# VectorE's order at the start of a fused attention and feed-forward block: tile 1's scaled x and tile 6's statistics change places

## The chip, the cores and the metric

The kernel runs on one core of a Trainium2 chip. The metric is the device time of one execution in microseconds (us), as the median of several timed runs. One more execution is recorded by the hardware profiler; its rows are the source of every other time below. The engines are called as the profile calls them: PE (TensorE, matrix products), DVE (VectorE), ACT (ScalarE), POOL (GpSimd) and SP (SyncE, which here only issues DMAs). PEld is the loading of weights into PE. Every engine works through its own list of instructions in order, and waits where an operand of another engine or of a DMA has not been signalled yet.

## The reference: what is computed

The input x has 2048 rows (tokens) of 512 values, in bfloat16. It is normalised over each row, and two branches of the normalised rows are added to x:

```python
xn = (x - mean(x)) / sqrt(var(x) + 1e-5)
# A: linear attention, 32 heads of 16
q, k, v = split(xn @ wqkv)                     # wqkv 512 x 1536
phi = lambda t: where(t > 0, t + 1, exp(t)) + 1e-6
kv  = sum over tokens of phi(k)^T v            # per head, 16 x 16
z   = sum over tokens of phi(k)
o   = phi(q) kv / (phi(q) . z + 1e-6)
A   = o @ wo                                   # wo 512 x 512
# B: gated feed-forward
B   = (silu(xn @ w_gate) * (xn @ w_up)) @ w_down   # inner width 1792
out = x + A + B
```

## The kernel before, in words

The 2048 rows are 16 tiles of 128 rows (`t` = 0 to 15). There are three stages. In the first, the head and a loop over tiles, every tile gets its statistics (mean and variance), its normalised rows, its k and q products, and the feature phi(k), called `pk`; a running product of xn and `pk` over all tiles is kept in four banks of the PE's accumulator memory (`gtacc`, L624). In the second, those sums are turned into the matrices that attention needs. In the third, the feed-forward products and the output tiles are worked through, in four chunks of 512 rows. The change touches the head alone, which ends near 17 us of 209.6; the loop over tiles from 5 on follows it.

Nothing plans the order. A small class, `_Prog`, keeps one list per engine: each call of a helper appends instructions to the list of its engine, in the order in which the calls stand in the source, and works out from the names read and written which semaphores must be waited for. So the order of calls in the source, written out by hand, is the order in which each engine works.

The helpers that matter here, by engine:

- DVE: `bns(t)` (L299) takes a tile's statistics and `agg(t)` (L302) makes mean and variance of them (`mv`). `xc_full(t)` (L426) subtracts the mean from x. `xn_dve(t)` (L316) makes the scaled x, that is (x - mean) * rstd, for tile t (`xn_sb`); `xn(t)` is the same followed, for t of 3 and more, by a DMA transpose of it on SP's queue (L463), which gives `xnT`. `clip_k(t)` (L539) clips the exponential of k. `first_feat(t)` (L588) adds it to the positive part `kpos` and writes the feature `pk`; for tiles from 4 on `maxadd_k(t)` (L548) does this from the accumulator bank.
- POOL: `eps(t)` and `rstd_of(t)` (L327, L336) add the epsilon to the variance and raise it to the power of -1/2; `eps_two(t)` and `rstd_two(t)` (L344, L353) do so for tiles t and t+1 in one instruction each. `feat_pool(0)` (L581) writes tile 0's feature, and `zsum(t)` (L612 for tile 0, L616 for the others) adds up the features over tiles, in float32.
- ACT: `first_ek`, `first_pk` and `first_pq` (L556, L562, L574) read the products of the first four tiles from the banks, scaled by `rstd`, as exponential of k, positive part of k (`kpos`) and q; `exp_k` (L520) is the exponential from tile 4 on.
- PE: `proj_part` and `proj_first` (L499, L486) form the products of the first four tiles, whose x is only centred and not scaled; `kproj` and `qproj` (L472) those of tiles 4 to 15, from `xnT`; `gtacc(t)` (L624) needs tile t's scaled x as weights and its feature as the other operand.

x arrives in single tiles up to tile 5, and in pairs from tile 6 on (6 and 7 together, then 8 and 9, and so on). Two waits are put into POOL's list on purpose: `zsum(0, [("xn", 3)])` starts only after tile 3's scaled x, and `zsum(1, [("xn", 7)])` only after tile 7's.

Of the kernel before, what the change touches and what calls it, by code (L numbers as in the profile page):

```python
# [109 lines left out]
def bass_parallel_sum__linear_attn_block__swiglu_ffn__prompt_kernel(  # L110
# [13 lines left out]
    pe, act, dve, pool, sp = nc.tensor, nc.scalar, nc.vector, nc.gpsimd, nc.sync  # L124
    bf, f32 = dt.bfloat16, dt.float32

    with contextlib.ExitStack() as es:
# [76 lines left out]
        def xload(eng, h, t0, n, after=()):  # L204
            K.dma(
                eng, lambda: h.dma_start(x_sb[:, t0:t0 + n, :], rows(xin, t0, n)),
                r=list(after), w=[("x", t0 + i) for i in range(n)],
            )
# [89 lines left out]
        def bns(t):  # L298
            K.op("dve", lambda: dve.bn_stats(stats[:, t, :], x_sb[:, t, :]), r=[("x", t)], w=[("st", t)])  # L299

        def agg(t):
            K.op("dve", lambda: dve.bn_aggr(mv[:, t, :], stats[:, t, :]), r=[("st", t)], w=[("mv", t)])  # L302
# [10 lines left out]
        def xn_dve(t):  # L313
            K.op(
                "dve",
                lambda: dve.tensor_scalar(  # L316
                    out=xn_sb[:, t, :], in0=x_sb[:, t, :], scalar1=mv[:, t, 0:1], scalar2=rstd[:, t:t + 1],
                    op0=ALU.subtract, op1=ALU.mult,
                ),
                r=[("x", t), ("mv", t), ("rstd", t)], w=[("xn", t)],  # L320
            )

        def eps(t, eng):
            h = dve if eng == "dve" else pool
            K.op(
                eng,
                lambda: h.tensor_scalar(  # L327
                    out=vpe[:, t:t + 1], in0=mv[:, t, 1:2], scalar1=1e-5, scalar2=None, op0=ALU.add,
                ),
                r=[("mv", t)], w=[("vpe", t)],  # L330
            )

        def rstd_of(t):
            K.op(
                "pool",
                lambda: pool.tensor_tensor(out=rstd[:, t:t + 1], in0=vpe[:, t:t + 1], in1=nhalf[:, 0:1], op=ALU.pow),  # L336
                r=[("vpe", t), ("nhalf",)], w=[("rstd", t)],
            )

        def eps_two(t, eng):  # L340
            h = dve if eng == "dve" else pool
            K.op(
                eng,
                lambda: h.tensor_scalar(  # L344
                    out=vpe[:, t:t + 2], in0=mv[:, t:t + 2, 1], scalar1=1e-5, scalar2=None, op0=ALU.add,
                ),
                r=[("mv", t), ("mv", t + 1)], w=[("vpe", t), ("vpe", t + 1)],
            )

        def rstd_two(t):  # L350
            K.op(
                "pool",
                lambda: pool.tensor_tensor(  # L353
                    out=rstd[:, t:t + 2], in0=vpe[:, t:t + 2], in1=nhalf[:, :], op=ALU.pow,
                ),
                r=[("vpe", t), ("vpe", t + 1), ("nhalf",)], w=[("rstd", t), ("rstd", t + 1)],
            )
# [65 lines left out]
        def xc_full(t):  # L423
            K.op(
                "dve",
                lambda: dve.tensor_scalar(  # L426
                    out=xc_sb[:, t, :], in0=x_sb[:, t, :], scalar1=mv[:, t, 0:1], scalar2=None, op0=ALU.subtract,
                ),
                r=[("x", t), ("mv", t)], w=[("xc", t, 0), ("xc", t, 1)],
            )  # L430
# [29 lines left out]
        def transpose_dma(t):  # L460
            K.dma(
                "sp",
                lambda: sp.dma_start_transpose(out=xnT[:, :, t * P:(t + 1) * P], in_=xn_sb[:, t, :]),  # L463
                r=[("xn", t)], w=[("xnT", t)],
            )
# [15 lines left out]
        def proj_first(t, wname, h):  # L481
            lo, b = (D, kb(t)) if wname == "wk" else (0, qb(t))
            K.op(
                "pe",
                [
                    (lambda c=c: pe.matmul(  # L486
                        banks[b], xcT[:, NDC * t + c, :], wqkv_sb[:, c, lo:lo + D],
                        start=(c == 0), stop=(c == NDC - 1),
                    ))
                    for c in (2 * h, 2 * h + 1)  # L490
                ],
                r=[("xcT", t, i) for i in (2 * h, 2 * h + 1)] + [(wname, i) for i in (2 * h, 2 * h + 1)], w=[bk(b)],
            )

        def proj_part(t, wname, c, pos):
            lo, b = (D, kb(t)) if wname == "wk" else (0, qb(t))
            K.op(
                "pe",
                lambda: pe.matmul(  # L499
                    banks[b], xcT[:, NDC * t + c, :], wqkv_sb[:, c, lo:lo + D],  # L500
                    start=(pos == 0), stop=(pos == NDC - 1),
                ),
                r=[("xcT", t, c), (wname, c)], w=[bk(b)],
            )
# [49 lines left out]
        def first_ek(t):  # L554
            K.op(
                "act", lambda: act.activation(ek[:, t % NE, :], banks[kb(t)], ACT.Exp, scale=rstd[:, t:t + 1]),  # L556
                r=[bk(kb(t)), ("rstd", t)], w=[("ek", t % NE)],
            )

        def first_pk(t):  # L560
            K.op(
                "act", lambda: act.activation(kpos[:, t % NE, :], banks[kb(t)], ACT.Relu, scale=rstd[:, t:t + 1]),  # L562
                r=[bk(kb(t)), ("rstd", t)], w=[("kpos", t % NE)],
            )
# [7 lines left out]
        def first_pq(t):  # L572
            K.op(
                "act", lambda: act.activation(pkq[:, t, 1, :], banks[qb(t)], ACT.Identity, scale=rstd[:, t:t + 1]),  # L574
                r=[bk(qb(t)), ("rstd", t)], w=[("pq", t)],
            )
# [15 lines left out]
        def clip_k(t):  # L592
            clip(ek[:, t % NE, :], ("ek", t % NE))
# [14 lines left out]
        def zsum(t, after=()):  # L608
            pk = pkq[:, t, 0, :]
            after = list(after)  # L610
            if t == 0:
                K.op("pool", lambda: pool.tensor_copy(zacc[:, :], pk), r=[("pk", t)] + after, w=[("zacc",)])  # L612
            else:
                K.op(
                    "pool",
                    lambda: pool.tensor_tensor(out=zacc[:, :], in0=zacc[:, :], in1=pk, op=ALU.add),  # L616
                    r=[("pk", t), ("zacc",)] + after, w=[("zacc",)],
                )

        def gtacc(t):  # L620
            K.op(
                "pe",
                [
                    (lambda c=c: pe.matmul(  # L624
                        banks[4 + c], xn_sb[:, t, c * P:(c + 1) * P], pkq[:, t, 0, :],
                        start=(t == 0), stop=(t == NT - 1),
                    ))
                    for c in range(NDC)
                ],
                r=[("xn", t), ("pk", t)], w=[bk(4 + c) for c in range(NDC)],  # L630
            )
# [7 lines left out]
        def xn(t):  # L639
            xn_dve(t)  # L640
            if t >= 3:
                transpose_dma(t)
# [35 lines left out]
        first_ek(0)  # L678
        clip_k(0)
        xc_full(3)  # L680
        bns(4)
        proj_part(1, "wk", 0, 0)
        proj_part(1, "wk", 1, 1)
# [14 lines left out]
        agg(4)  # L698
        bns(5)
        agg(5)  # L700
        bns(6)
        agg(6)
        proj_part(0, "wq", 2, 2)
        proj_part(1, "wq", 2, 2)
        proj_part(0, "wq", 3, 3)
# [1 line left out]
        proj_part(1, "wq", 3, 3)  # L707
        proj_first(2, "wk", 0)
        proj_first(2, "wk", 1)
        eps_two(1, "pool")  # L710
        rstd_two(1)
        first_ek(1)
        clip_k(1)
        first_pq(1)
# [3 lines left out]
        gtacc(0)  # L718
        eps_two(3, "pool")
        rstd_two(3)  # L720
        eps_two(5, "pool")
        rstd_two(5)
        xn(4)
        xload("sp", sp, 12, 2)
        xn_dve(1)
        first_pk(1)
        first_feat(1)
        proj_first(3, "wk", 0)
# [5 lines left out]
        first_pk(2)  # L734
        first_feat(2)
        xn(5)
        xn(6)
        first_pq(2)
        proj_first(3, "wk", 1)
        first_ek(3)  # L740
# [3 lines left out]
        gtacc(1)  # L744
        gtacc(2)
        xn_dve(3)
        zsum(0, [("xn", 3)])
        bns(7)
        kproj(4)
# [374 lines left out]
```

## Time and profile before

| | |
|---|---|
| median of 3 timed runs | 210.42 us (210.40 to 210.62) |
| profiled execution, whole time | 210.88 us |
| its span, first to last instruction | 209.6 us |
| busy share of the span: PE, DVE, ACT, POOL | 99%, 57%, 34%, 34% |
| granted PE clock | 1.00 |

The profile's span begins with the first instruction; all positions are us from there. The whole time of the profiled execution has 1.28 us around the span. A row of the timeline gives the start, the length, the engine, the line of the kernel, the operation, the tile written and the tiles read, the shapes, and the count of instructions in the row; one row can hold several instructions of one kind that follow each other. A bracket at its end tells how long the engine had been idle before and what ended that. Instructions of DVE and ACT overlap a little: the next one starts some 0.08 us before the one ahead has been written out, so that the distance between two starts is shorter than the length. A PE row's end is modelled, and the distance of starts is the better measure there too.

### The profile page before, as it was taken

Reading aid. Unit: us, or ns where it says so; the run is one execution under the profiler, and the core shown is the slowest. Engines: PE = TensorE matmul, PEld = TensorE weight load, DVE = VectorE, ACT = ScalarE, POOL = GpSimd, SP = SyncE. Lnnn points to the kernel's source line nnn. Section 1 sums busy time; section 2 is a strip of 40 time slices with the busy share of each in tenths; the row PEclk is TensorE's granted clock in tenths of the full one; section 3 lists DMA queues with packets and bytes.
Section 4 is the critical chain, followed back from the end, with each engine's and each line's share of the span. In section 5 each row is a group of like instructions: output and inputs, shape, how many; then the busy total and the mean of one; then the engine's idle time right before and its main releaser. Section 6 shows DMA issues by size and latency. Waiting matters only on the chain.

```text
span 209.6 us, 2822 instructions
## 1 busy us (share of the span) xinstructions
PE 206.9 (99%) x1014; PEld 94.5 (45%) x1014; DVE 120.3 (57%) x246; ACT 71.3 (34%) x126; POOL 72.0 (34%) x90
## 2 busy tenths in 40 slices
PE   8999999999999999999999999999999999999996
PEld 3444444444444444444444444444444444444444
DVE  4989989335465874637355746365556535374122
ACT  6686666976543331302122312213031213121000
POOL 3526977658032443223141422240424132221200
DMA  6763644697797021010101110102011010110101
GB/s 201 225 179 71 127 78 100 175 377 240 192 359 68 2 46 26 29 25 25 50 2 50 28 25 25 50 0 53 2 48 25 27 28 25 46 32 25 50 28 50
DMA packets 30287, 16.84 MB, mean 80 GB/s; under 512 B 20928, under 2 KB 29632, under 8 KB 30272
## 3 DMA queue, kind: packets, MB, share of 16 engines
q1 hardware_dynamic: 29984, 16.39, 29.9%
q10 hardware_dynamic: 288, 0.26, 0.4%
q8 instruction: 8, 0.13, 0.3%
q14 instruction: 7, 0.06, 0.1%
HBM read 9.70 MB, written 2.10 MB: 56 GB/s over the span
## 4 chain that ended last, share of the span: by engine, by line
PE 97%; DMA 1%; DVE 1%; issue 0%
PE psum L821 46%; PE psum L1026 23%; PE psum L472 10%; PE psum L1015 7%; PE psum L624 7%; PE psum L499 2%; PE psum L486 2%; DMA x_sb<-in_A_x_dram 1%; PE psum L444 0%; DVE stats L299 0%; PE psum L928 0%; PE psum L410 0%; PE psum L951 0%; DVE xc_sb L380 0%; DVE out_sb L1039 0%
## 5 line engine op out<-in xcount | busy, mean ns | idle before, releaser
L836 ACT ACTIVATE sg<-psum 128x512 bf16<-128x512 f32 x56 | 33.4, 598 | 106.0 <-PE psum L821 103.6
L821 PE MATMUL psum<-xnT,wg_sb 128*128 128x512 bf16 x224 | 57.5, 379 | 0.0
L821 PE MATMUL psum<-xnT,wu_sb 128*128 128x512 bf16 x224 | 57.5, 379 | 0.0
L970 POOL TENSOR_TENSOR prod<-pkq,zb 128x512 f32<-128x512 bf16 x16 | 18.6, 1161 | 55.9 <-DVE pkq L548 55.9
L821 PEld LDWEIGHTS psum<-xnT,wu_sb 128*128 128x128 bf16 x224 | 21.9, 98 | 26.4
L821 PEld LDWEIGHTS psum<-xnT,wg_sb 128*128 128x128 bf16 x224 | 21.7, 98 | 26.2 <-issue 0.2
L1039 DVE TENSOR_TENSOR out_sb<-psum,x_sb 128x512 bf16<-128x512 f32 (+2 forms) x17 | 11.2, 660 | 35.9 <-PE psum L1026 35.9
L994 POOL TENSOR_TENSOR pqn<-pkq,rden 128x512 bf16<-128x512 bf16 x16 | 16.9, 1055 | 36.6 <-DVE rden L988 36.6
L842 DVE TENSOR_TENSOR pkq<-psum,sg 128x512 bf16<-128x512 f32 x28 | 19.2, 686 | 17.1 <-PE psum L821 14.7
L842 DVE TENSOR_TENSOR xn_sb<-psum,sg 128x512 bf16<-128x512 f32 x28 | 18.8, 671 | 14.2 <-PE psum L821 13.6
L1026 PE MATMUL psum<-wd_sb,xn_sb 128*128 128x512 bf16 (+2 forms) x126 | 25.7, 355 | 0.0
L1026 PE MATMUL psum<-wd_sb,pkq 128*128 128x512 bf16 x112 | 25.5, 379 | 0.0
L472 PE MATMUL psum<-wqkv_sb,xnT 128*128 128x512 bf16 x96 | 22.5, 379 | 0.0
L616 POOL TENSOR_TENSOR zacc<-zacc,pkq 128x512 f32<-128x512 f32 x15 | 17.3, 1155 | 5.0 <-DVE ek L539 4.6
L1026 PEld LDWEIGHTS psum<-wd_sb,xn_sb 128*128 128x128 bf16 x126 | 11.8, 98 | 12.5
L1026 PEld LDWEIGHTS psum<-wd_sb,pkq 128*128 128x128 bf16 x112 | 11.0, 98 | 13.2
L1015 PE MATMUL psum<-m_sb,eq 128*128 128x512 bf16 (+2 forms) x68 | 16.6, 366 | 0.0
L624 PE MATMUL psum<-pkq,xn_sb 128*128 128x512 bf16 x64 | 15.9, 379 | 0.0
L472 PEld LDWEIGHTS psum<-wqkv_sb,xnT 128*128 128x128 bf16 x96 | 9.4, 98 | 11.3
L978 DVE TENSOR_REDUCE den<-prod 128x32 f32<-128x512 f32 x16 | 10.9, 683 | 5.9 <-POOL prod L970 5.9
L299 DVE BATCH_NORM_STATS2 stats<-x_sb 128x6 f32<-128x512 bf16 x16 | 10.9, 679 | 3.3 <-DMA x_sb<-in_A_x_dram 3.3
L548 DVE SCALAR_TENSOR_TENSOR pkq<-pkq,eq 128x512 bf16<-128x512 bf16 x16 | 11.1, 693 | 0.6
(73 smaller groups left out, 139.3 us busy)
## 6 DMA issues: line engine op xcount, KB each, us to landing
out_dram<-out_sb SPq DMA_DIRECT2D x15, 128.0 KB, 1.7
wg_sb<-in_B_w_gate_dram SPq DMA_DIRECT2D x2, 896.0 KB, 8.2
wu_sb<-in_B_w_up_dram SPq DMA_DIRECT2D x2, 896.0 KB, 6.4
wd_sb<-in_B_w_down_dram SPq DMA_DIRECT2D x1, 1792.0 KB, 11.1
x_sb<-in_A_x_dram SPq DMA_DIRECT2D x5, 256.0 KB, 3.0
x_sb<-in_A_x_dram SPq DMA_DIRECT2D x5, 128.0 KB, 3.2
wqkv_sb<-in_A_wqkv_dram SPq DMA_DIRECT2D x5, 128.0 KB, 3.4
wqkv_sb<-in_A_wqkv_dram SPq DMA_DIRECT2D x1, 512.0 KB, 8.4
```

What stands on the lines that cost most here:

```text
L472: (lambda c=c: pe.matmul(banks[b], xnT[:, c, t * P:(t + 1) * P], wqkv_sb[:, c, lo:lo + D], start=(c == 0), stop=(c == NDC - 1),))
L548: lambda: dve.scalar_tensor_tensor(out=dst, in0=src, scalar=0.0, in1=e, op0=ALU.max, op1=ALU.add,),
L616: lambda: pool.tensor_tensor(out=zacc[:, :], in0=zacc[:, :], in1=pk, op=ALU.add),
L624: (lambda c=c: pe.matmul(banks[4 + c], xn_sb[:, t, c * P:(c + 1) * P], pkq[:, t, 0, :], start=(t == 0), stop=(t == NT - 1),))
L821: (lambda c=c: pe.matmul(banks[b], w_sb[:, c, fc * P:(fc + 1) * P], xnT[:, c, C * 512:(C + 1) * 512], start=(c == 0), stop=(c == NDC - 1),))
L836: lambda: act.activation(sg[:, j % NSG, :], banks[gb], ACT.Silu),
L842: lambda: dve.tensor_tensor(out=hT(C, fc), in0=banks[ub], in1=sg[:, j % NSG, :], op=ALU.mult,),
L970: lambda: pool.tensor_tensor(out=p, in0=pkq[:, t, 1, :], in1=zb[:, :], op=ALU.mult),
L994: lambda: pool.tensor_tensor(out=pqn[:, t % NPN, :].rearrange("p (i g h e) -> p g i h e", i=NB, g=NG, e=DH), in0=pkq[:, t, 1, :].rearrange ...
L1015: (lambda g=g: pe.matmul(dst, pqnT(t)[:, g, :], m_sb[:, g, lo:hi], start=(g == 0), stop=False,))
L1026: (lambda fc=fc: pe.matmul(dst, hT(C, fc)[:, jj * P:(jj + 1) * P], wd_sb[:, fc, lo:hi], start=False, stop=(fc == NFC - 1),))
L1039: lambda: dve.tensor_tensor(out=o, in0=src, in1=x_sb[:, t, lo:hi], op=ALU.add),
```

## The change

Four calls or groups of calls in the head move; no instruction's shape changes except that the factors of tiles 5 and 6, formed by one pair of POOL instructions on two tiles, become two pairs on one tile each.

- Tile 1's scaled x, `xn_dve(1)`, stood behind tile 4's scaled x. It now stands behind `xc_full(3)`. The factors that it needs, `eps_two(1)` and `rstd_two(1)`, are called just ahead of it; POOL's own order is not changed by that, since no other POOL call stands between the two places.
- Tile 6's statistics, `bns(6)` and `agg(6)`, stood behind those of tile 5. They now stand behind the features of tiles 1 and 2 and tile 5's scaled x, ahead of `clip_k(3)`.
- Tile 6's factor is formed there as well, by `eps(6)` and `rstd_of(6)`, and tile 5's by `eps(5)` and `rstd_of(5)` at the place where both were formed together.
- Tile 6's scaled x and its transpose, `xn(6)`, stood behind `xn(5)`. They now stand behind tile 3's scaled x, ahead of the statistics of tile 7.

DVE's list in that part, by tile (s statistics and aggregate, c centred x, x scaled x, k clip, f feature):

```
before: c3 s4 s5 s6 k1 x4 x1 f1 k2 x2 f2 x5 x6 k3 f3 x3 s7
after:  c3 x1 s4 s5 k1 x4 f1 k2 x2 f2 x5 s6 k3 f3 x3 x6 s7
```

```diff
--- before.py
+++ after.py
@@ -678,6 +678,9 @@
         first_ek(0)
         clip_k(0)
         xc_full(3)
+        eps_two(1, "pool")
+        rstd_two(1)
+        xn_dve(1)
         bns(4)
         proj_part(1, "wk", 0, 0)
         proj_part(1, "wk", 1, 1)
@@ -698,8 +701,6 @@
         agg(4)
         bns(5)
         agg(5)
-        bns(6)
-        agg(6)
         proj_part(0, "wq", 2, 2)
         proj_part(1, "wq", 2, 2)
         proj_part(0, "wq", 3, 3)
@@ -707,8 +708,6 @@
         proj_part(1, "wq", 3, 3)
         proj_first(2, "wk", 0)
         proj_first(2, "wk", 1)
-        eps_two(1, "pool")
-        rstd_two(1)
         first_ek(1)
         clip_k(1)
         first_pq(1)
@@ -718,11 +717,10 @@
         gtacc(0)
         eps_two(3, "pool")
         rstd_two(3)
-        eps_two(5, "pool")
-        rstd_two(5)
+        eps(5, "pool")
+        rstd_of(5)
         xn(4)
         xload("sp", sp, 12, 2)
-        xn_dve(1)
         first_pk(1)
         first_feat(1)
         proj_first(3, "wk", 0)
@@ -734,7 +732,10 @@
         first_pk(2)
         first_feat(2)
         xn(5)
-        xn(6)
+        bns(6)
+        agg(6)
+        eps(6, "pool")
+        rstd_of(6)
         first_pq(2)
         proj_first(3, "wk", 1)
         first_ek(3)
@@ -744,6 +745,7 @@
         gtacc(1)
         gtacc(2)
         xn_dve(3)
+        xn(6)
         zsum(0, [("xn", 3)])
         bns(7)
         kproj(4)
```

## The prediction

> **What bounds the kernel now.** I read the busy times first, then TensorE's own waits, then busy time by stage. Columns of the stage view: stretch, its length, then busy time and count for PE, PEld, DVE, ACT and POOL, the granted clock, DMA share and GB/s.
>
> ```profile
> PE 206.9 (99%) x1014; PEld 94.5 (45%) x1014; DVE 120.3 (57%) x246; ACT 71.3 (34%) x126; POOL 72.0 (34%) x90
> ```
> ```profile
> PE psum L271 <- PEq L1109: 0.8, 1, 0.8
> ```
> ```profile
> 4.26:8.45 4.19, 4.19 (x21) 2.16 (x22) 4.03 (x14) 2.69 (x7) 1.89 (x5) 1.00 0.96 285
> 8.45:17.30 8.85, 8.85 (x45) 4.13 (x44) 7.80 (x21) 6.68 (x13) 3.46 (x6) 1.00 0.66 169
> 17.30:25.07 7.77, 7.77 (x37) 3.53 (x36) 7.29 (x19) 5.51 (x10) 6.97 (x12) 1.00 0.41 86
> ```
>
> The second row is the whole list of PE's waits: one, at the start. From 8.45 us, where the change begins to act, PE is busy for all of each stage. As a busy PE need not be at its peak, I check its pace in the timeline (start, length, engine, line, tiles, shapes, count):
>
> ```profile
> 9.53 1.89 PE L486 MATMUL psum<-wqkv_sb,xcT 128*128 128x512 bf16 x8
> 11.26 1.03 PE L624 MATMUL psum<-pkq,xn_sb 128*128 128x512 bf16 x4
> ...
> 13.85 1.89 PE L624 MATMUL psum<-pkq,xn_sb 128*128 128x512 bf16 x8
> 15.57 1.89 PE L472 MATMUL psum<-wqkv_sb,xnT 128*128 128x512 bf16 x8
> 17.30 1.03 PE L624 MATMUL psum<-pkq,xn_sb 128*128 128x512 bf16 x4
> ...
> 19.89 1.03 PE L624 MATMUL psum<-pkq,xn_sb 128*128 128x512 bf16 x4
> 20.75 1.89 PE L472 MATMUL psum<-wqkv_sb,xnT 128*128 128x512 bf16 x8
> ```
>
> Start to start, 8 matmuls take 1.73 us and 4 take 0.86: 0.216 each, everywhere. So nothing moved on VectorE (DVE) after 8.4 us can remove a PE stall, as there is none. It can only add one, and the question is which operand comes closest to its matmul.
>
> **The change, part by part.** DVE's rows before the change (a bracket is the idle time ahead and its releaser):
>
> ```profile
> 8.04 0.35 DVE L426 TENSOR_SCALAR xc_sb<-x_sb,mv 128x512 bf16<-128x512 bf16 x1
> 8.69 0.69 DVE L299 BATCH_NORM_STATS2 stats<-x_sb 128x6 f32<-128x512 bf16 x1 [0.30 <-DMA x_sb<-in_A_x_dram]
> ...
> 10.31 0.66 DVE L299 BATCH_NORM_STATS2 stats<-x_sb 128x6 f32<-128x512 bf16 x1
> ...
> 11.10 0.26 DVE L539 TENSOR_SCALAR ek<-ek 128x512 bf16<-128x512 bf16 x1
> 11.28 0.73 DVE L316 TENSOR_SCALAR xn_sb<-x_sb,mv,rstd 128x512 bf16<-128x512 bf16 x2
> 11.97 0.69 DVE L588 TENSOR_TENSOR pkq<-kpos,ek 128x512 bf16<-128x512 f32 x1
> ...
> 13.73 0.73 DVE L316 TENSOR_SCALAR xn_sb<-x_sb,mv,rstd 128x512 bf16<-128x512 bf16 x2
> 14.82 0.29 DVE L539 TENSOR_SCALAR ek<-ek 128x512 bf16<-128x512 bf16 x1 [0.35 <-ACT ek L556]
> 15.40 0.69 DVE L588 TENSOR_TENSOR pkq<-kpos,ek 128x512 bf16<-128x512 f32 x1 [0.29 <-ACT kpos L562]
> 16.01 0.41 DVE L316 TENSOR_SCALAR xn_sb<-x_sb,mv,rstd 128x512 bf16<-128x512 bf16 x1
> 16.33 0.69 DVE L299 BATCH_NORM_STATS2 stats<-x_sb 128x6 f32<-128x512 bf16 x1
> ...
> 18.66 0.68 DVE L548 SCALAR_TENSOR_TENSOR pkq<-psum,ek 128x512 bf16<-128x512 f32 x1
> ...
> 25.10 0.29 DVE L539 TENSOR_SCALAR ek<-ek 128x512 bf16<-128x512 bf16 x1 [0.30 <-ACT ek L520]
> ...
> 34.07 1.23 DVE L316 TENSOR_SCALAR xn_sb<-x_sb,mv,rstd 128x512 bf16<-128x512 bf16 x1
> ```
>
> From them: a scaled x (L316) occupies DVE for 0.32 us in a sequence (16.01 to 16.33); statistics with their aggregate (L299, L302) for 0.79 (10.31 to 11.10).
>
> (1) Tile 1's scaled x goes behind the subtraction at 8.04, so it starts near 8.37, in a gap of 0.30 that waits for tile 4's x. If it runs freely it costs 0.02 (8.37 + 0.32 = 8.69). But GpSimd (POOL) is busy there:
>
> ```profile
> 8.28 1.16 POOL L581 TENSOR_TENSOR pkq<-kpos,ek 128x512 bf16<-128x512 f32 x1 [0.45 <-ACT kpos L562]
> 9.69 0.23 POOL L344 TENSOR_SCALAR vpe<-mv 128x2 f32<-128x2 f32 x1 [0.26 <-DVE mv L302]
> 10.00 0.71 POOL L353 TENSOR_TENSOR rstd<-vpe,nhalf 128x2 f32<-128x2 f32 x1
> ...
> 16.48 0.61 POOL L612 CAST zacc<-pkq 128x512 f32<-128x512 bf16 x1 [4.19 <-DVE xn_sb L316]
> ...
> 34.00 1.15 POOL L616 TENSOR_TENSOR zacc<-zacc,pkq 128x512 f32<-128x512 f32 x1
> ```
>
> At 34.07 the same L316 took 1.23 us, not 0.41: POOL's operation began 0.07 earlier, ended at 35.15, and L316 ended 0.15 later. So a scaled x that begins after a large POOL operation waits it out. At 8.37 POOL has been running since 8.28: tile 1 would end at 9.44 + 0.15 = 9.59 and release DVE some 0.08 before its end (0.41 long, 0.32 in sequence), at 9.51: 0.82 late. Bounds 0.02 and 0.82; I take 0.82, as the row is nearest in kind and lead.
>
> The Trainium skill, "SBUF — State Buffer", section "Who interferes with whom", states that VectorE's two-port modes and GpSimd exclude each other, and whoever issues first holds the shared pair for the whole instruction. The pair of rows at 34 us agrees (1.23 us); by that rule tile 1's scaled x is hit here, and the sum for PE, worked out next, is the same with the loss or without it.
>
> (2) Tile 6's statistics leave their place at 10.31: 0.79 comes back. The clip at 11.10 is then due at 11.10 + 0.82 - 0.79 = 11.13. Tile 4's scaled x follows, and needs tile 3/4's factors from POOL, which wait for tile 4's statistics: 10.00 + 0.71 + 0.82 = 11.53, so it starts near 11.6, 0.3 late. Tile 1's scaled x is no longer behind it (0.32 saved), so the features of tile 1 come up at about 11.95. They wait for ScalarE (ACT) anyway:
>
> ```profile
> 11.24 0.70 ACT L562 ACTIVATE kpos<-psum,rstd 128x512 f32<-128x512 f32 x1
> ...
> 14.68 0.68 ACT L562 ACTIVATE kpos<-psum,rstd 128x512 f32<-128x512 f32 x1
> ```
>
> kpos ends at 11.94, the features start at 11.97 as before. Cost at this point: nothing. If the cover were gone, the features of tile 1 would still end at 12.7 for matmuls at 13.85.
>
> Tile 4's transpose on SP's queue moves with its scaled x:
>
> ```profile
> 11.71 1.19 SPq L463 DMA_TRANSPOSE xnT<-xn_sb  x1
> ...
> 15.40 1.27 SPq L463 DMA_TRANSPOSE xnT<-xn_sb  x1
> ```
> ```profile
> DMA to landing us min/median/max: 2.4/2.6/4.5
> ```
>
> 11.71 + 0.3 + 2.6 = 14.6, for matmuls at 15.57: hidden with 0.9 left. The x load behind it on that queue (tiles 12 and 13) moves by 0.3; tile 5's transpose is not reached by this, as tile 5's scaled x stays at 13.73.
>
> (3) At 13.73 stood the scaled x of tiles 5 and 6. Tile 6's 0.32 goes, its statistics' 0.79 come: +0.47, against 0.35 idle ahead of the clip at 14.82 and 0.29 ahead of the features at 15.40. The clip moves to about 14.9, the features wait for kpos (14.68 + 0.68 = 15.36) as before. Cost: nothing. POOL gets two instructions more, since tiles 5 and 6 no longer share theirs; it was idle for 4.19 us ahead of 16.48. Tile 6's factor: statistics done near 14.95, plus 0.1, plus 1.02 (9.69 to 10.71) gives 16.07, in time for 16.33.
>
> (4) Tile 6's scaled x now stands behind tile 3's, at 16.33, and everything behind on DVE moves by 0.32, until idle time at 25.10 (0.30) takes it up. POOL's cast at 16.48 starts 0.15 after it, so here DVE is first and the cast waits. Behind it in order are the statistics of tiles 7 and 8, the clip, tile 7's scaled x and tile 4's features (18.66). Those feed the matmuls at 19.89, so they end at 18.66 + 0.68 + 0.32 = 19.66. What PE needs ahead of a matmul is seen in its weight loads:
>
> ```profile
> 11.99 0.10 PEld L486 LDWEIGHTS psum<-wqkv_sb,xcT 128*128 128x128 bf16 x1 [0.20 <-ACT kpos L562]
> ```
>
> That load waited for kpos (end 11.94), started 0.05 later, and its matmul, 0.13 after it, began at 12.12, on the 0.216 pace (11.26 + 0.86). So an operand ready 0.18 ahead costs nothing: 19.66 + 0.18 = 19.84, against 19.89. It fits by 0.05; two rounded readings could make it 0.1 of stall, and no gain is possible. I take 0.
>
> Tile 6's transpose, issued at 15.40, now goes at about 16.75 and lands near 19.35, for matmuls at 20.75. Behind it on SP stands tile 7's, whose own scaled x comes at 18.6 or later; the queue is free by 18.0. Hidden.
>
> Sum: 0 + 0 + 0 + 0 = 0, to +0.1. The profiled execution took 210.88 (span 209.6 and 1.28 around it), 0.46 more than the median of the timed runs, 210.42; a difference of zero carries over: 210.4.
>
> **The rivals.** (a) Slower: at 16.48 POOL's cast gets ahead of tile 6's scaled x. Then that ends at 17.09 + 0.15 = 17.24 and releases DVE at 17.16, 0.83 late against 16.33. Tile 4's features end at 19.34 + 0.83 = 20.17, their matmuls start at 20.35, a stall of 0.46: 210.88. It decides once DVE is over 0.37 late at 18.66. Against it: DVE's lead of 0.15, where at 34 us a lead of 0.07 won for POOL.
>
> (b) Slower: tile 6's later transpose meets a slow landing. With the longest of the row, 4.5, it lands at 21.25, matmuls at 21.43 instead of 20.75: 0.68, 211.1. The median of 2.6 speaks against it.
>
> (c) Faster: the head is bound by DVE in some way PE's rows hide, and the filled gaps count. They are 0.30 + 0.35 + 0.29 = 0.94: 209.5 at most. Against it: the even pace of 0.216.
>
> (d) Slower: the loss at 8.37 runs further than worked out, since POOL's next operations, which now stand at other times, catch tile 4's scaled x. Another 1.16 there would eat the 0.9 of its transpose: +0.26 or more, 210.7 to 210.9.
>
> The order is written out by hand, so that the change does not take place is no case.
>
> **How the numbers follow.** About 0.2% (0.42 us) is what a measurement can tell from no change. Forecast, within 0.2%: 0.66. Slower by over 0.2%: (a) 0.13, (b) 0.05, (d) 0.06, together 0.24. Faster by over 0.2%: (c) 0.10, all that I leave for what the rows can't show. The forecast is 210.4; the range runs from 210.1 (part of (c)) to 211.0 (all of (a) and (d)).
>
> **What the profile after would show.** Right: PE's only wait is the one at the start; matmuls of L624 at 13.85, 17.30 and 19.89 within 0.05 of now; the second L316 near 8.37, lasting 1.2 (or 0.4 if POOL waited instead); features at 11.97 and 15.40 unmoved; the L299 of 16.33 at 16.65. Wrong: a gap before the matmuls of 19.89 or 20.75, or the L316 behind 16.01 lasting 0.9.

## The result, and the profile after

| | before | changed |
|---|---|---|
| median | 210.37 us (6 runs, 209.93 to 210.62) | 211.12 us (6 runs, 210.88 to 211.46) |
| profiled execution, span | 210.88, 209.6 us | 211.46, 210.2 us |

The changed kernel takes 1.0041 of the time before, 95% interval 1.0028 to 1.0053: 0.75 us more. The forecast was 210.4, no change.

PE's own waits in the changed kernel, where before there was one row (lines behind the head carry numbers two higher in this source):

```profile
PE psum L271 <- PEq L1111: 0.8, 1, 0.8
PE psum L624 <- DVE pkq L548: 0.8, 1, 0.8
PE psum L499 <- ACT xcT L456: 0.3, 1, 0.3
PE psum L823 <- issue: 0.2, 1, 0.2
```

The second row is the stall, at the matmuls that need tile 4's features. The timeline of the changed kernel shows how it comes about:

```profile
10.79 1.03 PE L624 MATMUL psum<-pkq,xn_sb 128*128 128x512 bf16 x4
...
20.49 1.04 PE L624 MATMUL psum<-pkq,xn_sb 128*128 128x512 bf16 x4 [0.83 <-DVE pkq L548]
```
```profile
6.26 0.69 DVE L299 BATCH_NORM_STATS2 stats<-x_sb 128x6 f32<-128x512 bf16 x1 [0.44 <-DMA x_sb<-in_A_x_dram]
...
8.60 0.35 DVE L426 TENSOR_SCALAR xc_sb<-x_sb,mv 128x512 bf16<-128x512 bf16 x1
8.86 1.27 DVE L316 TENSOR_SCALAR xn_sb<-x_sb,mv,rstd 128x512 bf16<-128x512 bf16 x1
...
11.66 0.26 DVE L539 TENSOR_SCALAR ek<-ek 128x512 bf16<-128x512 bf16 x1
12.11 0.41 DVE L316 TENSOR_SCALAR xn_sb<-x_sb,mv,rstd 128x512 bf16<-128x512 bf16 x1 [0.18 <-POOL rstd L353]
12.43 0.68 DVE L588 TENSOR_TENSOR pkq<-kpos,ek 128x512 bf16<-128x512 f32 x1
...
15.67 0.69 DVE L588 TENSOR_TENSOR pkq<-kpos,ek 128x512 bf16<-128x512 f32 x1
16.28 1.23 DVE L316 TENSOR_SCALAR xn_sb<-x_sb,mv,rstd 128x512 bf16<-128x512 bf16 x2
17.43 0.68 DVE L299 BATCH_NORM_STATS2 stats<-x_sb 128x6 f32<-128x512 bf16 x1
...
19.75 0.68 DVE L548 SCALAR_TENSOR_TENSOR pkq<-psum,ek 128x512 bf16<-128x512 f32 x1
```
```profile
8.83 1.15 POOL L581 TENSOR_TENSOR pkq<-kpos,ek 128x512 bf16<-128x512 f32 x1 [0.45 <-DVE ek L539]
...
15.79 1.01 POOL L336 TENSOR_TENSOR rstd<-vpe,nhalf 128x1 f32<-128x1 f32 x1
16.76 0.61 POOL L612 CAST zacc<-pkq 128x512 f32<-128x512 bf16 x1
```
```profile
10.78 0.70 ACT L562 ACTIVATE kpos<-psum,rstd 128x512 f32<-128x512 f32 x1
...
14.21 0.68 ACT L562 ACTIVATE kpos<-psum,rstd 128x512 f32<-128x512 f32 x1
```

The two scaled x in the row of 16.28 one by one, from the view of their tile (shortest, middle and longest in ns, then the first and last start):

```profile
L316 DVE TENSOR_SCALAR xn_sb<-x_sb,mv,rstd x2: 407/543/679, 16.3 to 16.8; 128x512 bf16<-128x512 bf16 x2
```

Three things are to be seen. First, PE is early and DVE late: PE's matmuls of tile 0 start at 10.79 (11.26 before), DVE's centred x of tile 3 at 8.60 (8.04 before), as tile 2's x kept DVE waiting for 0.44 us. So the features of tile 1 start at 12.43 although `kpos` was there at 11.48, and those of tile 3 at 15.67 although it was there at 14.89: the idle time that ACT caused on DVE before is gone.

Second, tile 1's scaled x lasts 1.27 us beside POOL's feature of tile 0, which began 0.03 ahead of it (8.83, 8.86), and ends 0.15 after it (9.98, 10.13).

Third, the pair of scaled x at 16.28 (tiles 3 and 6) takes 1.23 instead of 0.73. The power that makes tile 6's factor started on POOL at 15.79, 0.12 after tile 3's features on DVE, and lasted 1.01 us, until 16.80; tile 6's scaled x waited for it and started at 16.83 (17.51 less its 0.68). POOL's cast had come right behind the power at 16.76, and the scaled x ended at 17.51, 0.14 after the cast (17.37). DVE goes on at 17.43, and tile 4's features end at 20.43, 0.06 ahead of the matmuls. PE's own pace, from 10.79, would have been there at 10.79 + 8.63 = 19.42 (8.63 is 11.26 to 19.89, the unbroken pace before): 1.07 us of waits in all, nearly all of it at tile 4's matmuls.

### The profile page after: what moved, and what is told of

Read it like the earlier page. It is cut to its first block, busy times and chain, and to the rows that moved or that the text cites. A ratio compares the mean times of both kernels' runs of the same rounds, so it can differ in the third digit from the quotient of the medians.

```text
span 210.2 us, 2805 instructions
## 1 busy us (share of the span) xinstructions
PE 205.2 (98%) x995; PEld 93.9 (45%) x1014; DVE 121.8 (58%) x246; ACT 71.3 (34%) x126; POOL 73.1 (35%) x92
## 4 chain that ended last, share of the span: by engine, by line
PE 88%; DVE 6%; DMA 2%; issue 1%; POOL 1%; SPq 1%
PE psum L823 46%; PE psum L1028 23%; PE psum L472 8%; PE psum L1017 7%; PE psum L624 5%; DMA x_sb<-in_A_x_dram 2%; DVE stats L299 2%; DVE xn_sb L316 1%; DVE pkq L588 1%; DVE pkq L548 1%; POOL rstd L336 0%; DVE mv L302 0%; DVE ek L539 0%; SPq L213 0%; POOL rstd L353 0%
## 5 line engine op out<-in xcount | busy, mean ns | idle before, releaser
L823 PE MATMUL psum<-xnT,wu_sb 128*128 128x512 bf16 x216 | 55.8, 379 | 0.4
L1041 DVE TENSOR_TENSOR out_sb<-psum,x_sb 128x512 bf16<-128x512 f32 (+2 forms) x17 | 11.2, 661 | 35.9 <-PE psum L1028 35.9
```

The source lines that it names most:

```text
L823: (lambda c=c: pe.matmul(banks[b], w_sb[:, c, fc * P:(fc + 1) * P], xnT[:, c, C * 512:(C + 1) * 512], start=(c == 0), stop=(c == NDC - 1),))
```

## The experiments

Theories. H1: the loss is tile 6's scaled x, which gets its factor late and then loses to the cast. H2: it is tile 1's scaled x beside POOL's feature. H3: at first, that only both together exceed the slack; from e5 on, that each makes DVE late and their lateness adds up. H4: what DVE's lateness costs depends on where PE's head ends in that execution. H5: the cost is fixed. Times are medians, the difference is to the kernel before run with them (210.37, 210.50 and 210.46 us in the three groups); intervals are of the ratio.

**e1_x1**, the first part alone:

```diff
         xc_full(3)
+        eps_two(1, "pool")
+        rstd_two(1)
+        xn_dve(1)
         bns(4)
...
         xn(4)
         xload("sp", sp, 12, 2)
-        xn_dve(1)
```

> The kernel before with one part of the change: tile 1's scaled x, with its factors, behind tile 3's subtraction; tile 6 as before. Theory H1 (the loss comes from tile 6's scaled x behind tile 3's: it waits for its own late factor, then POOL's cast gets in ahead of it): no more than 0.1 us over the kernel before, since idle time of 0.35 and 0.29 us on DVE takes up most of what the collision at 8.4 us costs; the L588 of 11.97 near 12.5, the L299 of 16.33 near 16.5. Rival H2 (the loss comes from tile 1's scaled x, which at 8.86 us lasted 1.27 us beside POOL's feature): +0.5 to +0.75 us, with a stall at the matmuls of 19.89. Rival H3 (only both parts together exceed the slack): 0 here and 0 to +0.3 in the next run.

Measured 210.86, +0.49, ratio 1.0023 (1.0007 to 1.0040). Timeline of this kernel:

```profile
8.39 1.28 DVE L316 TENSOR_SCALAR xn_sb<-x_sb,mv,rstd 128x512 bf16<-128x512 bf16 x1
```
```profile
10.43 1.03 PE L624 MATMUL psum<-pkq,xn_sb 128*128 128x512 bf16 x4
11.29 1.89 PE L486 MATMUL psum<-wqkv_sb,xcT 128*128 128x512 bf16 x8
13.23 2.16 PE L624 MATMUL psum<-pkq,xn_sb 128*128 128x512 bf16 x8
15.23 1.89 PE L472 MATMUL psum<-wqkv_sb,xnT 128*128 128x512 bf16 x8
```

The collision is there, and the loss with it, but not at the place that H2 named: the matmuls of tiles 1 and 2 take 2.16 instead of 1.89 and start 0.2 late, and none waits at tile 4. H1 alone is out, and so is H3 as it was first put, which had 0 here.

**e2_tile6**, the other parts alone (the changed kernel, with tile 1's scaled x back behind tile 4's):

```diff
         xc_full(3)
-        eps_two(1, "pool")
-        rstd_two(1)
-        xn_dve(1)
         bns(4)
...
         xload("sp", sp, 12, 2)
+        xn_dve(1)
```

> The changed kernel without that part: tile 1's scaled x stays behind tile 4's as before, tile 6's statistics, factor and scaled x are moved as in the change. H1: +0.6 to +0.8 us over the kernel before, as much as the whole change (+0.75), with the L316 behind tile 3's ending 0.15 us after POOL's cast. H2: 0 to +0.2. H3: 0 to +0.3.

Measured 210.68, +0.31, ratio 1.0010 (0.9997 to 1.0023): less than the whole, and not clear of nothing. Its timeline has the power and tile 3's features in the other order:

```profile
15.20 0.58 POOL L336 TENSOR_TENSOR rstd<-vpe,nhalf 128x1 f32<-128x1 f32 x1
```
```profile
15.23 0.69 DVE L588 TENSOR_TENSOR pkq<-kpos,ek 128x512 bf16<-128x512 f32 x1 [0.26 <-ACT kpos L562]
15.85 0.72 DVE L316 TENSOR_SCALAR xn_sb<-x_sb,mv,rstd 128x512 bf16<-128x512 bf16 x2
```

The power starts 0.03 ahead of the features and takes 0.58; the pair takes 0.72. What H1 saw in the changed kernel doesn't happen here. But PE's first matmuls with tile 0's features come 3.05 behind the centred x of tile 3 in this execution, and the changed kernel at such a distance (e7, below) has the same order: whether it happens without the first part where PE is earlier isn't shown.

**e3_x6_only**, tile 6's scaled x alone behind tile 3's:

```diff
         xn(5)
-        xn(6)
...
         xn_dve(3)
+        xn(6)
```

> The kernel before with tile 6's scaled x alone moved behind tile 3's; its statistics and its factor stay early. H1: tile 6's scaled x follows tile 3's at once and POOL's cast waits for it, DVE is 0.32 us late and not 0.83 or more, and the time is 0 to +0.2 us over the kernel before. If the move of the scaled x is dear by itself, and not its late factor: +0.6 or more.

Measured 210.50, +0.13, ratio 1.0002 (0.9989 to 1.0015). No cost can be measured for the place of the scaled x where its factor is early.

**e4_cast_behind_x6**, on the changed kernel:

```diff
-        zsum(0, [("xn", 3)])
+        zsum(0, [("xn", 6)])
```

> The changed kernel with POOL's cast (the first sum of features) made to wait for tile 6's scaled x instead of tile 3's. H1: the part of the loss that is the cast's goes: tile 6's scaled x ends 0.4 us after its factor and not 0.7, DVE gains 0.3 to 0.6 us there, and the time falls to +0.2 to +0.5 us over the kernel before. If the cast is not involved: +0.75 as the change.

Measured 210.81, +0.44, ratio 1.0018 (1.0008 to 1.0028). Its timeline:

```profile
15.69 1.01 POOL L336 TENSOR_TENSOR rstd<-vpe,nhalf 128x1 f32<-128x1 f32 x1
17.21 0.61 POOL L612 CAST zacc<-pkq 128x512 f32<-128x512 bf16 x1 [0.52 <-DVE xn_sb L316]
```
```profile
15.57 0.69 DVE L588 TENSOR_TENSOR pkq<-kpos,ek 128x512 bf16<-128x512 f32 x1
16.18 0.97 DVE L316 TENSOR_SCALAR xn_sb<-x_sb,mv,rstd 128x512 bf16<-128x512 bf16 x2
```

The late power stays (1.01, begun 0.12 after the features), the cast's part goes: the pair takes 0.97 instead of 1.23. The gain, 0.31 of 0.75, is as expected; the intervals of the two kernels touch.

**e5_feat_behind_x1**, on the changed kernel:

```diff
         # feat_pool
-                r=[("kpos", t % NE), ("ek", t % NE)], w=[("pk", t)],
+                r=[("kpos", t % NE), ("ek", t % NE), ("xn", 1)], w=[("pk", t)],
```

> The changed kernel with POOL's feature of tile 0 (the operation of 8.3 to 9.4 us) made to wait for tile 1's scaled x, so that this cannot lose to it. The two parts alone cost +0.49 and +0.31 us, near the +0.75 of the whole. Theory H3a (their lateness on DVE adds up, and the collision is what makes the first part dear): tile 1's scaled x takes 0.4 instead of 1.27 us, the first part's share goes, +0.2 to +0.35 us over the kernel before remain. Rival: the collision is made up for by the statistics taken out, as the prediction had it, and the time stays at +0.6 to +0.8.

Measured 210.83, +0.33, ratio 1.0019 (1.0008 to 1.0031): as H3 has it from here on. Tile 1's scaled x took 0.41 us; the power took 0.58 and the pair 0.72 with it, though PE's matmuls of tile 0 stood no later behind the centred x of tile 3 (2.84) than in an execution of the changed kernel with the late power (2.93, l1 below). So at this distance it is the collision that brings the late power about.

**e9_x1_feat**, the first part alone (e1) with the same wait on POOL:

> The kernel before with tile 1's scaled x behind tile 3's subtraction, tile 6 as before, and POOL's feature of tile 0 made to wait for that scaled x. If the whole cost of the first part (+0.49 us when done alone) is the collision with that feature, it goes, and the gap of 0.3 us ahead of tile 4's statistics is used: -0.3 to +0.1 us against the kernel before. If the part is dear by its place, or the collision only passes on to POOL's next operations: +0.3 to +0.5.

Measured 210.50, +0.04, ratio 0.9993 (0.9971 to 1.0015), against +0.49 without the wait. Its timeline:

```profile
8.99 0.41 DVE L316 TENSOR_SCALAR xn_sb<-x_sb,mv,rstd 128x512 bf16<-128x512 bf16 x1
```
```profile
9.55 1.16 POOL L581 TENSOR_TENSOR pkq<-kpos,ek 128x512 bf16<-128x512 f32 x1 [1.03 <-DVE xn_sb L316]
```

PE lost 0.05 from tile 0's matmuls to tile 4's, where e1 lost 0.49, though PE was no later against DVE (2.10 behind the centred x, 2.31 in e1). So the collision is the cost of the first part, and POOL can bear to be the one that waits; the intervals of e1 and e9 overlap a little, so this rests on the rows. POOL's later power for tiles 5 and 6 took 1.28 instead of 0.71 here and held nothing up. No gain from the gap can be measured.

**e11_after_both**, the changed kernel with the waits of e4 and e5:

> The changed kernel with both orders on POOL changed: tile 0's feature behind tile 1's scaled x, and the cast behind tile 6's scaled x. With the first alone +0.33 us remained. If what remained is the cast ahead of tile 6's scaled x: 0 to +0.15 us. If it is the place of tile 6's statistics and scaled x (0.32 us and the wait for the factor): +0.2 to +0.35.

Measured 210.70, +0.24, ratio 0.9997 (0.9976 to 1.0017). With e5 at +0.33 this fits the second reading, that what remains is DVE's 0.32 us; but the interval, from 0.5 below the kernel before to 0.4 above it, excludes neither reading, nor zero.

**e6_before_late_pe** and **e7_after_late_pe**, four unused matmuls ahead of tile 2's transposes, in the kernel before and in the changed one:

```diff
         first_pk(0)
+        K.op("pe", [(lambda: pe.matmul(banks[6], cw, cx, start=True, stop=True)) for _ in range(4)],
+             w=[bk(6)])
         tp_first(2, 0, 4)
```

> The kernel before with four matmuls of 512 columns put into PE's list ahead of tile 2's transposes (into a free bank, results not used): PE and what hangs on it start 4 x 0.216 = 0.86 us later against DVE. Theory H4 (a slack: what PE's list holds up to 8.4 us ends at another time from run to run, DVE's lateness costs only where PE is early): +0.6 to +0.9 us over the kernel before, less 0.86 only by what the kernel before already lost in stalls or in waits for weights. To be read with the next run.

> The changed kernel with the same four matmuls. H4: the later start covers DVE's lateness, so this is only 0 to +0.2 us above the kernel before with the four matmuls (instead of +0.75), that is +0.6 to +1.1 us over the kernel before. Rival H5 (the change costs a fixed amount wherever PE stands): +0.75 above that kernel, +1.35 to +1.65 over the kernel before.

Measured 210.98, +0.48 (1.0028; 1.0017 to 1.0039), and 211.26, +0.76 (1.0041; 1.0026 to 1.0057). The four matmuls cost the kernel before 0.48, less than expected, and the changed kernel 0.14 (its median was 211.12 in another group). Between the two kernels 0.28 is left instead of 0.75, where H4 had 0 to 0.2: the later PE covers most of the loss. H5 had 1.35 to 1.65 for the changed kernel, which the interval (up to 1.2) excludes. e7's timeline:

```profile
8.35 0.35 DVE L426 TENSOR_SCALAR xc_sb<-x_sb,mv 128x512 bf16<-128x512 bf16 x1
8.61 1.27 DVE L316 TENSOR_SCALAR xn_sb<-x_sb,mv,rstd 128x512 bf16<-128x512 bf16 x1
...
15.74 0.69 DVE L588 TENSOR_TENSOR pkq<-kpos,ek 128x512 bf16<-128x512 f32 x1 [0.26 <-ACT kpos L562]
16.35 0.72 DVE L316 TENSOR_SCALAR xn_sb<-x_sb,mv,rstd 128x512 bf16<-128x512 bf16 x2
```
```profile
11.60 1.03 PE L624 MATMUL psum<-pkq,xn_sb 128*128 128x512 bf16 x4
...
20.23 1.03 PE L624 MATMUL psum<-pkq,xn_sb 128*128 128x512 bf16 x4
```

This is the execution that the prediction described: the collision at 8.61, the features held by ACT again, the pair of 0.72, and 8.63 from tile 0's matmuls to tile 4's, without a stall.

**e8_after_stat8** and **e10_before_stat8**, tile 8's statistics behind tile 4's features, on the changed kernel and on the kernel before:

```diff
         rstd_of(7)
-        stat(8)
...
         maxadd_k(4)
+        stat(8)
         bns(9)
```

> The changed kernel with tile 8's statistics (0.8 us on DVE) moved from ahead of tile 4's clip to behind tile 4's features. H3a with the stall at the matmuls that wait for tile 4's features (20.49 in the profile of the changed kernel, 0.83 us): those features come 0.8 us earlier, that stall goes, and +0.0 to +0.3 us over the kernel before remain, from stalls at the features of tiles 1 and 2. Rival (the loss lies further ahead, at the features of tiles 1 and 2): +0.6 to +0.75 as the change.

> The kernel before with tile 8's statistics moved behind tile 4's features, as was tried on the changed kernel, where tile 7's scaled x then waited 0.46 us for its factor and the stall passed on to the features of tile 5. If the kernel before already loses time at tile 4's features in a typical execution (its median is 0.5 us under its profiled execution, with PE earlier by as much and DVE not): -0.3 to 0 us. If it passes on here as well: +0.1 to +0.5.

e8 is a miss: 211.56, +1.06, ratio 1.0047 (1.0032 to 1.0061). Its timeline:

```profile
19.02 0.41 DVE L316 TENSOR_SCALAR xn_sb<-x_sb,mv,rstd 128x512 bf16<-128x512 bf16 x1 [0.46 <-POOL rstd L336]
```
```profile
20.09 1.04 PE L624 MATMUL psum<-pkq,xn_sb 128*128 128x512 bf16 x4 [0.24 <-DVE pkq L548]
...
23.24 1.04 PE L624 MATMUL psum<-pkq,xn_sb 128*128 128x512 bf16 x4 [0.39 <-DVE pkq L548]
```

The statistics had covered the time in which POOL makes tile 7's factor; without them DVE idles 0.46, the stall at tile 4 shrinks and a second one comes at tile 5. On the kernel before the same edit gave 210.40, -0.06, ratio 0.9988 (0.9967 to 1.0009): no sign that tile 4's features bound it, though the interval would hide a few tenths.

**More executions** of the same kernels, one profile each: the changed kernel twice (l1, l2), the kernel before twice (e12, l3), and e1's kernel (l4).

> The changed kernel once more, one look. Theory H4: the matmuls of tile 4's features start at the later of two times, 8.63 us behind those of tile 0 (PE's pace of 0.216 us), or 0.06 us behind the end of tile 4's features on DVE. In the first profile of this kernel the second was 1.0 us later than the first. Where PE's matmuls of tile 0 start before 11.2 us, a wait of 0.2 to 1.1 us is seen in all, at the features of tiles 1, 2 or 4; the whole time is 210.9 to 211.5. Rival H5 (a fixed cost): the same wait wherever PE starts.

> The same once more, for another start of PE: a wait of 0.2 to 1.1 us in all if the matmuls of tile 0 start before 11.2, none over 0.2 if they start after 11.5.

> The kernel before once more, for another profiled execution. Theory H4: PE's transposes of tile 2 start anywhere from 7.6 to 8.5 us (8.45 in the first profile), from the arrival of weights and x; where they start early, PE shows waits for features of DVE in this kernel too, and the slack of 0.05 us that the prediction found at 19.89 is gone. Rival: the slack moves with PE, and no wait on DVE is seen.

> The kernel before once more, one look: in both profiles so far tile 4's features ended 0.3 to 0.55 us before PE would take them, and no matmul waited for DVE. H4: again 0.2 us or more of slack there, and no wait for DVE, wherever PE starts.

> The kernel before with tile 1's scaled x moved alone, once more, one look: scaled x again near 1.25 us long beside POOL's feature of tile 0; if PE's matmuls of tile 0 start before 10.9, waits for the features of tiles 1 and 2 of 0.1 to 0.5 us in all, as in its first profile (0.49); if later than 11.2, none.

The rows of the two executions of the changed kernel, l1 then l2:

```profile
8.43 0.35 DVE L426 TENSOR_SCALAR xc_sb<-x_sb,mv 128x512 bf16<-128x512 bf16 x1
```
```profile
11.36 1.03 PE L624 MATMUL psum<-pkq,xn_sb 128*128 128x512 bf16 x4
...
20.33 1.04 PE L624 MATMUL psum<-pkq,xn_sb 128*128 128x512 bf16 x4 [0.17 <-DVE pkq L548]
```
```profile
8.09 0.35 DVE L426 TENSOR_SCALAR xc_sb<-x_sb,mv 128x512 bf16<-128x512 bf16 x1
```
```profile
10.64 1.03 PE L624 MATMUL psum<-pkq,xn_sb 128*128 128x512 bf16 x4
...
20.00 1.04 PE L624 MATMUL psum<-pkq,xn_sb 128*128 128x512 bf16 x4 [0.56 <-DVE pkq L548]
```

And e12, the kernel before once more:

```profile
8.79 0.35 DVE L426 TENSOR_SCALAR xc_sb<-x_sb,mv 128x512 bf16<-128x512 bf16 x1
...
18.34 0.68 DVE L548 SCALAR_TENSOR_TENSOR pkq<-psum,ek 128x512 bf16<-128x512 f32 x1
```
```profile
10.71 1.03 PE L624 MATMUL psum<-pkq,xn_sb 128*128 128x512 bf16 x4
...
19.67 1.03 PE L624 MATMUL psum<-pkq,xn_sb 128*128 128x512 bf16 x4
```
```profile
9.16 1.29 SPq L435 DMA_TRANSPOSE xcT<-xc_sb  x1
```
```profile
11.78 1.42 PEld L486 LDWEIGHTS psum<-wqkv_sb,xcT 128*128 128x128 bf16 x8 [0.54 <-ACT kpos L562]
```

In the table, PE's lead is the time from the start of DVE's centred x of tile 3 (L426) to PE's first matmul with tile 0's features; the next column goes from that L426 to the matmuls of tile 4's features; the last is what PE lost between the two groups of matmuls, against 8.63.

| profiled execution | PE's lead | L426 to tile 4's matmuls | lost |
|---|---|---|---|
| before | 3.22 | 11.85 | 0 |
| before (l3) | 3.23 | 11.86 | 0 |
| before (e12) | 1.92 | 10.88 | 0.33 |
| changed | 2.19 | 11.89 | 1.07 |
| changed (l2) | 2.55 | 11.91 | 0.73 |
| changed (l1) | 2.93 | 11.90 | 0.34 |
| changed, PE later (e7) | 3.25 | 11.88 | 0 |

In the three executions of the changed kernel tile 4's matmuls come 11.9 us behind the centred x wherever PE stands: they hang on DVE, whose features of tile 4 end 0.06 to 0.07 ahead of them. In e7 the 11.88 is PE's pace; the features ended 0.23 earlier (20.00). In the kernel before these matmuls come when PE gets there, 10.88 in the one execution with a short lead. DVE's own way tells what the change cost it: from the centred x of tile 3 to the end of tile 4's features it took 11.83 in the changed kernel (8.60 to 20.43) and 10.23 in e12 (8.79 to 19.02), for the same instructions. Of these 1.60 us, 0.86 are the collision (1.27 instead of 0.41), 0.18 the wait for tile 4's factor and 0.50 the pair (1.23 instead of 0.73).

H4 had waits for DVE's features in e12, and there are none; the 0.33 lost there came earlier. The list of waits names ACT's `kpos` at two weight loads, but `kpos` had ended 0.39 ahead of the first (10.69 to 11.39, load at 11.78). What ended just ahead of it is the DMA transpose of tile 3's centred x, issued at 9.16 behind L426 and landed 2.5 us later, at 11.66. The second load (15.33) follows the transpose of tile 4's scaled x in the same way (12.07 and 3.2 to landing: 15.27). So a late DVE seems to have cost the kernel before something too, by another road.

The bounds of 11.2 and 11.5 that l1 and l2 were given, on PE's start alone, were the wrong measure: l1 started at 11.36 and still lost 0.34, as DVE was late too. In l4 (lead 2.37) e1's loss showed again, 0.42 at the matmuls of tiles 1 and 2.

Both engines make the lead. DVE waited 0.61 us for tile 3's x in e12 and 0.44 for tile 2's in the first profile of the changed kernel, and for neither in the first profile. On PE, the first twelve matmuls of L499 took 3.52 to 3.54 in the three executions of the two kernels with the longest leads (the first profile, l3 and l1) and 2.75 in e12. In the first profile their first four started 0.43 apart, twice the later distance, at a granted clock of 1.00 and with no wait for a DMA in the list; why is open.

No version beat the kernel before by more than its interval.

## Why the prediction was wrong

**What bounds the kernel.** Right as read, PE's even pace, but read from one execution with a lead of 3.22. That is the step that failed: the cover named for parts 2 and 3 ("They wait for ScalarE (ACT) anyway") and the 0.05 of part 4 were properties of that lead, and "a difference of zero carries over" took them to every execution. The prediction did ask what comes if the cover is gone, but only for tile 1's matmuls; it didn't carry DVE's lateness on to part 4, where it put tile 6's late factor and the cast. The prediction had noted that this execution was 0.46 over the median and made nothing of it. In the three profiles of the changed kernel, with leads of 2.19 to 2.93, the cover was gone and PE lost 0.34 to 1.07. e7, with a lead of 3.25, did what the prediction said.

**Part 1, the collision.** Right: 0.82 late was forecast, the scaled x took 1.27 to 1.28 in every profile of a kernel that has it (0.41 with the wait of e5, e9 and e11). The margin was smaller than forecast: POOL was 0.02 to 0.03 ahead in these profiles, not 0.09. The lower bound of 0.02 is 0 by its own sum (8.37 + 0.32 = 8.69). The reading that it costs nothing held for the lead of 3.25; alone, in e1, it cost 0.49.

**Part 2, the statistics taken out.** Its sum was right to 0.05: from the centred x to the clip 3.09 forecast and 3.06 measured (8.60 to 11.66), to tile 4's scaled x 3.56 and 3.51 (12.11), with the forecast wait for POOL (0.18 measured). The cover was wrong: `kpos` was 0.95 earlier than the features of tile 1.

**Part 3, tile 6's factor.** Wrong by its last sentence. From the end of the statistics to the factor 1.12 was forecast; it took 1.41 (15.39 to 16.80), since the power lasted 1.01 and not 0.71. I applied the exclusion of POOL and DVE to scaled x and cast, and not to the small power beside tile 3's features. In nine profiles of kernels with tile 6's late factor it goes by the order: begun 0.11 to 0.12 after the features, the power lasted 1.01 (the changed kernel three times, e4, e8); begun 0.03 to 0.04 before them, 0.58 (e2, e5, e7, e11). In the second group DVE stood idle just before, waiting for ACT, and the idle time lets the power go first. A start ahead of the features is not enough where DVE is busy: in e1, e9 and l4 the common power of tiles 5 and 6 began 0.02 to 0.03 ahead of tile 1's features, while tile 4's scaled x still ran, and lasted 1.48, 1.28 and 1.27 instead of 0.71. e1's row:

```profile
12.46 1.48 POOL L353 TENSOR_TENSOR rstd<-vpe,nhalf 128x2 f32<-128x2 f32 x1
```

The Trainium skill, "SBUF — State Buffer", section "Who interferes with whom", names this case as well: an instruction of VectorE with two SBUF inputs, as these features are, contends with a GpSimd instruction that reads SBUF, and issue order decides who waits. The five profiles with the features first agree. In the four with the power first nobody waited that the rows show: the features took 0.69 to 0.70 there, as elsewhere.

**Part 4, the cast.** Wrong on who is first, as the scaled x waited for its factor while the cast was queued right behind the power. Rival (a) had the price, 0.83 from 16.33: from tile 3's features to tile 7's statistics it is 1.76 now (15.67 to 17.43) and was 0.93 (15.40 to 16.33). That the price fits so well is luck. Rival (a) had 0.32 for the place and 0.51 for the cast; with the cast held back (e4) the same stretch is still 1.49 (15.57 to 17.06), so the cast's part is 0.27, and 0.24 are the late power, which rival (a) didn't have. In l1 tile 4's matmuls start at 20.33 and rival (a) had 20.35; that is luck too: tile 3's features start 0.11 later there than before (15.51, 15.40), and the matmuls follow tile 4's features by 0.06 where the prediction allowed 0.18. Its mechanism was right in the main, its condition was missed, and its chance of 0.13 was too low. The place of the stall was as named; its size was 0.34 to 1.07 and not 0.1. At the lead of the first profile the slack was larger than 0.05, as an operand needs to be ready 0.06 to 0.07 ahead there and not 0.18: in e7 tile 4's features end 11.65 behind the centred x, where 11.62 was forecast (8.04 to 19.66), and PE doesn't wait.

**The rest.** Tile 6's later transpose (rival b) cost nothing that shows: its products follow tile 4's features as before (20.49 to 21.37, before 19.89 to 20.75). Rival (d) didn't come: tile 4's scaled x took 0.41 (12.11). The gain of rival (c) shows nowhere: e9 fills the first gap without the collision, and its interval reaches from 0.6 below the kernel before to 0.3 above it, which speaks against the 0.94 but not against a few tenths.

The three profiled executions of the changed kernel (211.46, 211.33, 210.97) lie 0.49 on the mean over the three of the kernel before (210.88, 210.64, 210.77), the timed medians 0.75 apart. That most timed executions have a short lead would fit, but isn't shown: they carry no rows. Nor is the share of each part in the 0.75 exact: 0.49 and 0.31 have intervals of 0.3 us to each side.

## What to carry to other kernels

A slack read from one execution is the slack of that execution: where an engine's start varies from execution to execution, read several profiles before counting on a cover, above all if the profiled one is slower than the median. When an instruction is moved, place each engine's neighbours in time beside it: on DVE and POOL a start 0.03 or 0.12 us earlier or later decided here who waited out the other, and even a power over one column held up a chain. If an early place collides, a wait given to the engine with slack can remove the cost (e9), though a filled gap is worth nothing unless the engine bounds the stage. And when a wait is put down to something that ended long before, look for what ended just before: in e12 that was a DMA.

## What was not expected of the hardware

A POOL power on one value per partition lasted 0.58 us when begun just before DVE's features, with DVE idle, and 1.01 when begun after them. It ended at 16.80, after tile 3's scaled x as well (16.28 to 16.69). But the 0.43 more is less than what was left of the features when it began (15.79 to 16.36), so that the scaled x held it too isn't shown. And the start of PE's first features against DVE's centred x varied between 1.9 and 3.2 us from execution to execution of the kernel before, whose whole time in those three lay between 210.64 and 210.88.
